# Reordering blocks, transposes, weight loads and the FFN ramp in an attention + softplus-FFN kernel

## Chip, core and metric

The kernel runs on one NeuronCore of a Trainium2 chip. The metric is the device time of one execution in microseconds (us); lower is better. Most executions of one kernel agree within a per cent; the medians below include slow ones. "Span" is the time from the first to the last instruction that the profile records; it is 1.7 to 2.9 us shorter than the device time of the same execution.

Engines: PE is TensorE (PEld its weight loads), DVE is VectorE, ACT is ScalarE, POOL is GpSimd, SP is SyncE, which here only issues DMAs. A trailing q (SPq, POOLq) is that engine's DMA-issuing queue.

## The reference

Attention with 8 heads over 4 sequences of 768 tokens, a causal band of 96 tokens plus 8 global tokens, an ALiBi-like distance bias, then a two-layer FFN with softplus between the layers.

```python
scores = scale * np.matmul(q, k.transpose(0, 1, 3, 2))       # q, k, v: [4, 8, 768, 64] f32
keep = is_global | is_local                                   # 8 globals, 96 back
scores = np.where(keep, scores - slopes * dist, -1e9)
a = softmax(scores)
x = np.matmul(a, v)                                           # -> [3072, 512]
h = x @ w_in                                                  # [512, 2048]
g = np.maximum(h, 0.0) + np.log1p(np.exp(-np.abs(h)))         # softplus
out = g @ w_out                                               # [2048, 512] -> [3072, 512]
```

The kernel works in blocks of 128 tokens (24 in all, 6 per sequence). Block i of a sequence needs the keys and values of blocks i and i-1 and the 8 global tokens of block 0 of the same sequence. Two blocks make one FFN group of 256 tokens; a group has 8 slots, each with eight w_in matmuls of 256 columns ("mm1") and four w_out matmuls of 512 columns ("mm2").

## The kernel before

Loads, casts and the order of the start (cuts are marked):

```python
def load(w):                       # two blocks of one sequence
    nc.sync.dma_start(q32[:], q[b, :, sl, :].rearrange("h (p r) d -> p h (r d)", r=2))
    nc.sync.dma_start(k32[:], k[b, :, sl, :].rearrange("h (p r) d -> p h (r d)", r=2))
    # ... v in four DMAs of 64 partitions

def transp(w, which, psum, eng):   # q and k: eight PE transposes, then one copy
    for r in range(2):
        for m in range(NPAIR):
            nc.tensor.transpose(tr[:, m, r, :], src[:, r, 2 * m : 2 * m + 2, :]..., ident[:])
    cast_on[eng](t[:], psum.rearrange("p (a b t) -> p b a t", b=2, t=64))

def weights(s):                    # DMA with cast f32 -> bf16, issued by GpSimd
    nc.gpsimd.dma_start(w_in_bf[:, :, c], moe_w_in[:, c]...)
    nc.gpsimd.dma_start(w_out_bf[:, f * s : f * s + f, :], moe_w_out[...]...)

load(0); load(1)
# ... biases, casts, transposes, scores of blocks 0 and 1
weights(0)
# ... transposes and scores of blocks 2 and 3
load(2)
for s in range(1, NS):
    weights(s)
load(3)
# ... then one static list: per FFN slot mm1, mm2, and pieces of attention between them
```

x_transp transposes the attention output by four PE transposes per block. All blocks of sequence 0 come first, then those of sequence 1, and so on.

The softmax here doesn't subtract the row's maximum and nothing guards it: scores larger than these inputs give would overflow.

## Time and profile before

The time before is 260.86 us (median of 4; 259.65 to 260.95). The profiled execution had a span of 256.0 us.

From the profile page of the kernel before: busy time, and the rows of the span in 40 slices of 6.4 us. A digit is tenths of the slice that the engine was busy; in the row PEclk it is tenths of full TensorE clock.

```profile
span 256.0 us, 5170 instructions
...
PE 225.1 (88%) x2144; PEld 154.6 (60%) x2144; DVE 139.1 (54%) x279; ACT 156.2 (61%) x201; POOL 34.9 (14%) x66
...
PE   1437687399999999999999999999999999999991
...
PEclk9999999689999999999999999999999999999998
DMA  7999999999965095192291590300202003003033
```

The same kernel in stretches of 20 us; columns are window, its length, busy us of each engine with instruction counts, granted clock, DMA share, GB/s.

```profile
0.00:20.00 20.00, 6.48 (x64) 4.71 (x64) 11.76 (x36) 8.63 (x10) 5.70 (x15) 1.00 1.11 228
20.00:40.00 20.00, 14.85 (x146) 10.64 (x147) 12.08 (x23) 9.91 (x14) 8.10 (x11) 1.00 1.22 217
40.00:60.00 20.00, 13.95 (x123) 9.30 (x122) 6.40 (x13) 8.52 (x12) 3.83 (x7) 0.83 1.18 228
60.00:80.00 20.00, 19.66 (x207) 14.13 (x206) 13.43 (x26) 16.01 (x22) 2.35 (x4) 1.00 0.89 193
```

The chain of waits between 15 and 50 us, in order of time (start, length, what), cut to its two longest pieces:

```profile
23.91 3.47 SPq L102
...
30.44 17.32 DMA v_338<-in_v_dram
```

What to read: from 60 us on PE is full, so there only PE's own work counts. Before 60 us PE was busy for 35.3 of 60 us, part of that at half clock (the clock record shows 0.5 from 46.2 to 53.0 us). The costliest link of the start is one v load, issued at 30.4 us, landing after 17.3 us: it shares the DMA engines with the weights. In the full part two blocks repeat every 17.81 us (mean over the groups from 70.30 to 177.15 us, by the start of each group's first mm1).

### The profile page before, as it was taken

The page shows a single profiled execution, that of the slowest core. Times are in us where ns is not written, and L with a number is a line of the kernel's source. Part 1 is how long each engine was busy: PE and PEld are TensorE (multiplying, and loading weights), DVE is VectorE, ACT ScalarE, POOL GpSimd, SP SyncE. Part 2 cuts the span into 40 slices and gives each one's busy share as a digit, 9 for nine tenths or more (in the row PEclk, how much of TensorE's full clock was granted, in tenths as well). Part 3 has the DMA queues.
Part 4 walks back from the last instruction along what each step waited for, and adds up shares of the span by engine and source line. Part 5 has one row for each costly group of instructions (what it writes and reads, how often), then busy time and mean ns, then how long its engine had stood idle before and what let it go on. Part 6 is the DMA issues. An engine that isn't in the chain of part 4 may idle for free.

```text
span 256.0 us, 5170 instructions
## 1 busy us (share of the span) xinstructions
PE 225.1 (88%) x2144; PEld 154.6 (60%) x2144; DVE 139.1 (54%) x279; ACT 156.2 (61%) x201; POOL 34.9 (14%) x66
## 2 busy tenths in 40 slices
PE   1437687399999999999999999999999999999991
PEld 1324465177667677666776766676676667666640
DVE  6475832246674865764665757746656757430012
ACT  2455544087876767767665777766577677766600
POOL 2142810130300300303001103030000000000000
PEclk9999999689999999999999999999999999999998
DMA  7999999999965095192291590300202003003033
GB/s 188 250 250 199 257 197 199 245 233 240 178 177 105 5 244 86 41 242 48 64 240 30 127 203 0 85 0 22 63 3 65 20 1 86 0 3 82 0 82 82
DMA packets 58391, 29.69 MB, mean 116 GB/s; under 512 B 26624, under 2 KB 55296, under 8 KB 58368
## 3 DMA queue, kind: packets, MB, share of 16 engines
q1 hardware_dynamic: 54144, 25.17, 45.5%
q0 software_dynamic: 4224, 4.19, 9.7%
q8 instruction: 16, 0.26, 0.5%
q14 instruction: 7, 0.06, 0.1%
HBM read 27.26 MB, written 6.29 MB: 131 GB/s over the span
## 4 chain that ended last, share of the span: by engine, by line
PE 79%; DMA 9%; ACT 3%; SPq 3%; DVE 3%; issue 1%; DVEq 0%; POOL 0%; POOLq 0%
PE o_ps_349 L251 17%; PE h_ps_348 L225 16%; PE o_ps_350 L251 16%; PE h_ps_347 L225 15%; DMA v_338<-in_v_dram 7%; PE s_ps L163 4%; PE tr_ps L126 3%; SPq L102 2%; DMA k_84<-in_k_dram 2%; PE tr_ps L214 2%; PE s_ps L165 2%; PE x_ps L195 2%; PE x_ps L198 2%; DVE z L172 1%; ACT g L239 1%
## 5 line engine op out<-in xcount | busy, mean ns | idle before, releaser
L225 PEld LDWEIGHTS <-w_in_bf 128*128 128x128 bf16 x768 | 73.2, 99 | 22.0 <-DVE XT L217 0.7
L172 DVE TENSOR_TENSOR z<-s_ps,biasA 128x1024 f32<-128x1024 f32 x38 | 46.4, 1220 | 26.1 <-PE s_ps L165 26.0
L251 PE MATMUL o_ps_349<-w_out_bf,g 128*128 128x512 bf16 x192 | 57.7, 383 | 1.1 <-ACT g L239 0.7
L251 PE MATMUL o_ps_350<-w_out_bf,g 128*128 128x512 bf16 x192 | 57.6, 382 | 0.0
L179 ACT ACTIVATE pb<-z 128x1024 bf16<-128x1024 f32 (+1 forms) x48 | 46.8, 975 | 14.4 <-DVE z L172 13.2
L237 ACT ACTIVATE e<-h_ps_348 128x512 f32<-128x512 f32 x48 | 28.6, 596 | 40.8 <-PE h_ps_348 L225 40.8
L251 PEld LDWEIGHTS <-g 128*128 128x128 bf16 x384 | 35.1, 98 | 29.8 <-issue 1.7
L225 PE MATMUL h_ps_347<-XT,w_in_bf 128*128 128x256 bf16 x384 | 51.5, 279 | 0.5 <-DVE XT L217 0.5
L239 ACT ACTIVATE g<-e 128x1024 bf16<-128x1024 f32 x48 | 50.7, 1057 | 1.5
L225 PE MATMUL h_ps_348<-XT,w_in_bf 128*128 128x256 bf16 x384 | 50.8, 276 | 0.0
L237 ACT ACTIVATE e<-h_ps_347 128x512 f32<-128x512 f32 x48 | 28.3, 589 | 22.2 <-PE h_ps_347 L225 22.0
L260 DVE COPY osb<-o_ps_349 128x512 f32<-128x512 f32 x12 | 8.3, 692 | 24.1 <-PE o_ps_349 L251 23.6
L202 DVE RECIPROCAL rcp<-x_ps 128x4 f32<-128x4 f32 x46 | 8.1, 176 | 24.4 <-PE x_ps L198 24.4
L203 DVE TENSOR_TENSOR xs<-x_ps,rcp 128x256 bf16<-128x256 f32 x46 | 19.5, 425 | 1.6
L148 POOL COPY kT<-kT 128x32 bf16<-128x32 bf16 x16 | 3.4, 213 | 121.0 <-PE s_ps L165 116.4
L126 PE MATMUL tr_ps<-ident,qb 128*128 128x128 bf16 x96 | 8.6, 242 | 11.7 <-DVE qb L113 11.7
L163 PE MATMUL s_ps<-qT,kT 64*128 64x128 bf16 x180 | 16.2, 231 | 2.8 <-ACT kT L134 2.2
L165 PE MATMUL s_ps<-qT,kT 64*128 64x128 bf16 x152 | 13.8, 228 | 5.5 <-POOL kT L148 5.5
L195 PE MATMUL x_ps<-vb,pb 128*128 128x65 bf16 x156 | 15.5, 198 | 1.3 <-DVE xs L203 1.3
L163 PEld LDWEIGHTS <-kT 64*128 64x128 bf16 x192 | 8.6, 99 | 12.3 <-issue 8.2
L198 PE MATMUL x_ps<-vb,pb 128*128 128x65 bf16 x156 | 15.4, 198 | 0.6 <-DVE vb L154 0.6
L134 DVE COPY qT<-tr_ps 128x1024 bf16<-128x1024 bf16 x11 | 7.6, 692 | 13.3 <-PE tr_ps L126 13.2
(86 smaller groups left out, 181.0 us busy)
## 6 DMA issues: line engine op xcount, KB each, us to landing
out_dram<-osb SPq DMA_DIRECT2D x48, 128.0 KB, 2.4
w_in_bf<-in_moe_w_in_dram POOLq DMA_DIRECT2D x4, 512.0 KB, 11.9
w_out_bf<-in_moe_w_out_dram POOLq DMA_DIRECT2D x4, 512.0 KB, 14.6
q_82<-in_q_dram SPq DMA_DIRECT2D x1, 512.0 KB, 4.2
k_84<-in_k_dram SPq DMA_DIRECT2D x1, 512.0 KB, 6.1
v_86<-in_v_dram SPq DMA_DIRECT2D x4, 128.0 KB, 5.0
q_91<-in_q_dram SPq DMA_DIRECT2D x1, 512.0 KB, 5.5
k_93<-in_k_dram SPq DMA_DIRECT2D x1, 512.0 KB, 7.0
```

Of the source, the lines that this page charges most:

```text
L126: nc.tensor.transpose(tr[:, m, r, :], src[:, r, 2 * m : 2 * m + 2, :].rearrange("p a b -> p (a b)"), ident[:],)
L163: nc.tensor.matmul(psum[:, reg_base(lh), :], kt_of(n)[rows, m, :], qT[rows, m, :])
L165: nc.tensor.matmul(psum[:, reg_base(lh) + 1, :], kt_of(n - 1)[rows, m, :], qT[rows, m, :])
L172: nc.vector.tensor_tensor(z[:], psum[:, :, :], biasA[:, half, :, :], ALU.add)
L179: nc.scalar.activation(pb[:, 0:nr, :], z[:, 0:nr, :], AF.Exp, scale=1.0 / root_d)
L195: nc.tensor.matmul(xv[:, lh, :], pb[:, 2 * j, :], vb_of(n)[:, h, :], start=True, stop=False)
L198: nc.tensor.matmul(xv[:, lh, :], pb[:, 2 * j + 1, :], vb_of(n - 1)[:, h, :], start=False, stop=True)
L203: nc.vector.tensor_tensor(xs[:, 4 * half : 4 * half + 4, :], xv[:, :, 0:D], rcp[:][:, :, None].to_broadcast([P, 4, D]), ALU.mult,)
L225: nc.tensor.matmul(hv[:, j, :], w_in_bf[:, m, fb * P : fb * P + P], XT[:, m, W * g : W * g + W], start=(m == 0), stop=(m == NM - 1),)
L237: nc.scalar.activation(e[:, p % 2, :].rearrange("p (j t) -> p j t", j=2), hv, AF.Exp)
L239: nc.scalar.activation(state["g", g][:, 2 * p - 2 : 2 * p + 2, :].rearrange("p a t -> p (a t)"), e[:].rearrange("p a t -> p (a t)"), AF.Ln ...
L251: nc.tensor.matmul(o_ps[ns][:], gt[:, fb, ns * P : ns * P + P], w_out_bf[:, fb, :], start=(fb == 0), stop=(fb == NFB - 1),)
```

## The change

Its intent: have FFN work for PE early, and take work off PE later.

1. **Block order.** The first blocks of all four sequences lead: they have no predecessor block and give two FFN groups before the rest. Their tokens come in units (sequence 0), (sequence 1), (2 and 3).
2. **Transposes.** q, k and x of the early units stay on PE; later ones are DMA transposes issued by SyncE.
3. **One FIFO ring.** Weights are read as f32 by SyncE into the same 12 raw slots as the tokens, one DMA after another, and GpSimd casts them. Half of each load of the first two units still goes through ScalarE's queue. Loads of later units are held back by manual waits (`gates`) on a given mm1 slot.
4. **mm2 ramp.** The first two groups' mm2 accumulate in three PSUM banks; the later groups use one, and the kernel before used two.
5. **Around it.** A planner fixes the order of every engine from guessed durations; 90 filler matmuls of 256 columns stand where PE would idle at the start; the bias of the first blocks is added by PE; scores of the two head parities alternate.

The core of the diff (a planner of some 130 lines and many renamings are cut):

```diff
+FIRST_UNITS = [[0], [1], [2, 3]]
+FIRST_LOADS = "u0 u1 u2 i0 i1 i2 i3 i4 i5 i6 i7 o0 u3 o1 o2 o3 o4 o5 o6 o7".split()
+FILLERS = 90
+ACT_UNITS = 2
+PE_KEYS = {0: (("s", 2), ("s", 3)), 1: (("s", 2), ("s", 3)), 2: (("s", 2), ("s", 3)), 3: (("s", 0), ("s", 1))}
+PE_X = {0: ("o",), 1: ("o",), 2: ("o",), 3: ("o",), 4: ("x",), 5: ("x",)}
+O_KEYS = {(0, 1): ("s", 3), (1, 0): ("s", 2)}
+ENG_W = {}
 ...
-        nc.gpsimd.dma_start(
-            w_in_bf[:, :, c], moe_w_in[:, c].rearrange("(m p) c -> p m c", p=P)
-        )
+                return nc.sync.dma_start(
+                    raw_t[slot][:].rearrange("p (m c) -> p m c", m=NM),
+                    moe_w_in[:, W * p : W * p + W].rearrange("(m p) c -> p m c", p=P),
+                )
 ...
+        def cast():                               # eng is GpSimd unless ENG_W says otherwise
+                copy_on[eng](w_in_bf[:, :, W * p : W * p + W], raw_t[slot][:]...)
 ...
+            return nc.sync.dma_start_transpose(dst[:, 0 : cols // P, :], src)      # q, k
 ...
+                return nc.sync.dma_start_transpose(dst, xs[:].rearrange("p h d -> p (h d)"))
 ...
-            nc.vector.tensor_copy(vb_of(n - 1)[sl, :, 0:D], vb_of(first)[sl, :, 0:D])
+                nc.gpsimd.tensor_copy(vb_of(prev)[sl, :, 0:D], vb_of(first)[sl, :, 0:D])
 ...
+            if (g, p) in marks:
+                gates[which, i] = [marks[g, p]]   # load of unit i waits for mm1 of group g, slot p
```

## The prediction

> **What bounds the kernel now.** The busy table gives PE 88% of 256.0 us; the measured time is 4.9 us longer. In stretches of 20 us PE is full from 60 to 240 us (19.7 to 20.0). Before that it is busy 6.5, 14.9 and 14.0 us. The chain of waits says why: k load, cast, transpose, bias, one unit after another, then a 17.3 us v DMA landing at 48 us, sharing the engines with weights issued late from GpSimd (17 to 29 us). PE then runs at half clock for some 7 us (clock row 0.6 and 0.8 near 50 us).
>
> Two blocks then repeat every 17.95 us: FFN 8 x (0.87 + 0.87) = 13.9, attention 4.05: q/k transposes 2 x 0.445, x transposes 2 x 0.22, scores about 4 x 0.43, PV. ScalarE has 13.3 us of work in it.
>
> **What changes.**
> - PE loses 144 of 192 q/k and 72 of 96 x transposes: 216 x 0.0555 = 12.0 us. It gains 8 bias matmuls of 512 columns (1.7). Scores of both head parities alternate row halves and share one switch: estimate 2 to 3 less. Sum -13 us, all critical. 90 fillers (0.11 each) fall into start-up idle and hold the clock.
> - Two blocks: 17.95 becomes about 16.4 us; ScalarE at 13.3 (81%) is not yet the bound.
> - 40 DMA transposes join SyncE's queue. The Trainium skill, "DMA: Bandwidth & Descriptors", "Latency and other measured facts", gives them 261 GB/s: about 1 us for 128x1024 bf16; no trace here shows one. The DMA row is at a half near 100 us, a fifth near 200.
> - Start: 3.1 MB for the first blocks, then w_in, one unit, w_out: 13.1 MB in one ring. 512 B packets take 27 to 33 ns per engine (250 to 300 GB/s), weight packets 96 ns per 2 KB read (341 GB/s). So first mm1 at about 16 us, w_in complete at 28, w_out at 42 to 46. Two groups give 1.75 us of PE work per slice of about 1.6 us, so PE stays nearly fed. Instruction order times these durations: 201 us of PE work with switches, 5 of it before the first mm1. Idle until then 11, waits for weights about 5, later holes about 3.
> - Tail: last store split: 4.5 instead of 5.3 us.
>
> 201 + 11 + 5 + 3 + 4.5 = 224 span, + 4.9 = 229; I say **228 us**, 8 in 10 within **220 to 238**. Faster by over 2%: 0.96; within 2%: 0.03; slower: 0.01. Of the 33 us gained, about 13 are PE work, 19 start-up idle and cold clock, 1 tail.
>
> **What would show it.** First w_in matmul at 15 to 18 us; PE full by 30 us without a clock dip; last w_out slice at 41 to 48 us; two blocks every 16.2 to 16.8 us between 80 and 170 us; scores and mm1 waiting under 1 us in total per group on DMA transposes; PE end at 215 to 220.
>
> **What would make it wrong.** DMA transposes slower than estimated (landing 6 us or more, or issue 2 us or more), so that SyncE's in-order queue holds up loads, XT and stores; f32 weights at 250 GB/s; GpSimd weight casts (1.04 us, beside v casts) pacing mm1; ScalarE's exp with permuted output over 0.6 us, making ScalarE the bound; a static order whose guesses miss, with PE holes of 0.5 us per slot.

## The result and the profile after

The changed kernel takes 236.12 us (median of 4 executions: 234.42, 234.59, 237.66 and one of 239.18). Executions over 1.5% slower than the fastest of the same kernel are left out of the means. The ratio to the kernel before is 0.9055, with a 95% interval of 0.8986 to 0.9124. Ratios here are the mean time of one kernel's fast runs over that of the other's fast runs of the same rounds, so they are not quite the ratio of the medians quoted beside them. The change is faster by 9.5%; the predicted 228 us lay 8 us too low, within the range.

The page of the kernel after (slices of 5.8 us):

```profile
span 232.6 us, 5037 instructions
...
PE 214.6 (92%) x1994; PEld 149.0 (64%) x2026; DVE 113.1 (49%) x219; ACT 154.9 (67%) x202; POOL 98.1 (42%) x178
...
PE   8979889898995998999999999999999999999883
...
PEclk9999999999998899999999999999999999999998
DMA  5999999999796449868877545899679422110021
```

The same kernel in stretches of 20 us, columns as before:

```profile
0.00:20.00 20.00, 16.84 (x161) 12.99 (x163) 12.74 (x41) 6.55 (x14) 8.99 (x23) 1.00 0.96 224
20.00:40.00 20.00, 18.07 (x185) 14.47 (x186) 7.75 (x22) 15.29 (x23) 11.58 (x13) 1.00 1.11 344
40.00:60.00 20.00, 18.12 (x153) 11.19 (x154) 10.88 (x19) 10.21 (x13) 16.84 (x27) 1.00 1.03 266
60.00:80.00 20.00, 17.11 (x175) 10.49 (x176) 11.30 (x18) 13.23 (x16) 9.31 (x19) 0.91 0.81 202
```

The 16.84 us of the first stretch are not what they seem: most are fillers. Counting each matmul at the spacing it has at full rate (an estimate of mine: 0.0555 us for 128 columns, 0.109 for 256, 0.2155 for 512, about 0.03 for the small attention ones), PE did 4.4 us of useful work and 9.8 us of filling before 21 us. In the kernel before the same count gives 22.3 us of useful work in the first 60 us; after, 35.8 (two bias matmuls that this trace lacks are counted in). That is the 13.5 us gained at the start.

Three things in the trace stand against the prediction:

- The first mm1 starts at 21.17 us, not at 15 to 18.
- There is a new hole near 70 us, and half clock follows it. The clock record of this execution shows 0.5 from 73.78 to 77.19 us.
- Device time minus span is 1.8 us, not 4.9.

The hole, in the timeline of GpSimd and of PE (start, length, engine, line, operation, tiles; in brackets the idle time before and who ended it). L395 casts loaded rows, L501 copies the values of the global tokens into block n-1's tile, L704 is mm2:

```profile
69.22 0.21 POOL L492 COPY kT<-kTf 128x32 bf16<-128x32 bf16 x1
70.70 1.27 POOL L395 CAST vb<-raw 64x512 bf16<-64x512 f32 x2 [1.27 <-DMA raw<-in_v_dram]
72.01 1.26 POOL L501 COPY vb<-vb 4x512 bf16<-4x512 bf16 x2
73.33 1.27 POOL L395 CAST vb<-raw 64x512 bf16<-64x512 f32 x2
```

```profile
73.53 4.44 PE L704 MATMUL o_ps<-w_out_bf,g 128*128 128x512 bf16 x12
```

The waits of PE between 60 and 80 us in the same kernel (waiting for; us in total, times, longest):

```profile
PE x_ps L601 <- POOL vb L501: 1.3, 1, 1.3
PE x_ps L598 <- ACT g L683: 0.7, 1, 0.7
PE s_ps L546 <- DVE z L572: 0.7, 1, 0.7
```

PE's PV matmuls needed the copy at 72.01, which stood behind a v cast in GpSimd's static order, and that cast waited for a v load that landed at 70.64 us. PE lost 2.7 us in three waits between 69 and 73.3 us; only the last and longest is put down to the copy, the other two to ScalarE and VectorE. Then twelve mm2 matmuls took 4.44 us instead of the 12 x 0.2155 = 2.6 us of full rate.

### The profile page after: what moved, and what is told of

Same layout as the page of the kernel before. It is cut to its first block, busy times and chain, and to the rows that moved or that the text cites. A ratio compares the mean times of both kernels' runs of the same rounds, so it can differ in the third digit from the quotient of the medians.

```text
span 232.6 us, 5037 instructions
## 1 busy us (share of the span) xinstructions
PE 214.6 (92%) x1994; PEld 149.0 (64%) x2026; DVE 113.1 (49%) x219; ACT 154.9 (67%) x202; POOL 98.1 (42%) x178
## 4 chain that ended last, share of the span: by engine, by line
PE 78%; DMA 7%; DVE 4%; POOL 3%; issue 3%; ACT 3%; DVEq 0%; POOLq 0%; ACTq 0%
PE o_ps L704 30%; PE h_ps L657 29%; PE s_ps L546 5%; PE h_ps L807 5%; DMA raw<-in_k_dram 4%; PE s_ps L704 3%; DMA raw<-in_v_dram 3%; PE x_ps L601 2%; ACT pb L581 2%; PE x_ps L598 2%; DVE z L572 2%; POOL vb L501 2%; POOL vb L395 1%; DVE osb L728 1%; PE s_ps L443 1%
## 5 line engine op out<-in xcount | busy, mean ns | idle before, releaser
L657 PE MATMUL h_ps<-XT,w_in_bf 128*128 128x256 bf16 x768 | 95.5, 273 | 1.5 <-POOL w_in_bf L350 0.9
L704 PE MATMUL o_ps<-w_out_bf,g 128*128 128x512 bf16 x323 | 84.8, 385 | 4.0 <-DVE osb L728 1.6
L672 ACT ACTIVATE e<-h_ps 128x512 f32<-128x512 f32 x96 | 59.9, 630 | 30.9 <-PE h_ps L657 30.3
L704 PEld LDWEIGHTS <-g 128*128 128x128 bf16 x384 | 35.9, 99 | 36.2 <-issue 7.0
L581 ACT ACTIVATE pb<-z 128x1024 bf16<-128x1024 f32 x40 | 41.8, 1050 | 18.9 <-DVE z L572 18.8
L395 POOL CAST vb<-raw 64x512 bf16<-64x512 f32 (+1 forms) x60 | 32.8, 547 | 23.1 <-DMA raw<-in_v_dram 17.5
L728 DVE COPY osb<-o_ps 128x512 f32<-128x512 f32 (+1 forms) x23 | 15.2, 665 | 51.4 <-PE o_ps L704 51.3
L395 POOL CAST kb<-raw 64x512 bf16<-64x512 f32 (+1 forms) x44 | 24.0, 545 | 17.5 <-DMA raw<-in_k_dram 15.9
L501 POOL COPY vb<-vb 4x512 bf16<-4x512 bf16 x32 | 19.5, 610 | 17.1 <-PE x_ps L601 16.0
L598 PEld LDWEIGHTS <-pb 128*128 128x128 bf16 x160 | 12.5, 98 | 5.2 <-issue 1.9
L546 PE MATMUL s_ps<-qT,kT 64*128 64x128 bf16 x288 | 13.4, 217 | 0.7 <-DVE z L572 0.7
L601 PEld LDWEIGHTS <-pb 128*128 128x128 bf16 x160 | 11.3, 97 | 3.4 <-issue 1.0
## 6 DMA issues: line engine op xcount, KB each, us to landing
out_dram<-osb SPq DMA_DIRECT2D x23, 256.0 KB, 2.4
```

What stands on the lines that cost most here:

```text
L395: copy_on[eng](dst, src[64 * x : 64 * x + 64, r, :, :])
L501: nc.gpsimd.tensor_copy(vb_of(prev)[sl, :, 0:D], vb_of(first)[sl, :, 0:D])
L546: nc.tensor.matmul(s_ps[:, reg, :].rearrange("p (r t) -> p r t", r=2), kt[rows, m, :], qv(rows, m), start=not biased, stop=True, skip_grou ...
L581: nc.scalar.activation(pb[:, 0:nr, :], src, AF.Exp, scale=1.0 / root_d)
L598: nc.tensor.matmul(xv[:, m, :], pb[:, 2 * m, :], vb_of(n)[:, h, :], start=True, stop=False)
L601: nc.tensor.matmul(xv[:, m, :], pb[:, 2 * m + 1, :], vb_of(prev)[:, h, :], start=False, stop=True)
```

## Experiments

The knobs named in the diffs are constants of the changed kernel. One caution holds for all of them: the order of every engine is planned from durations, so a small edit also moves other instructions. The hole at 70 us hangs on this: between 60 and 84 us PE's longest wait for the global-v copy is 1.04 to 2.72 us with half clock after it in after_again, e2, e3 and e5, and at most 0.3 us, without half clock, in e1, e4, e8 and, with the copies on VectorE, e7 (e11 has no such wait at all, e12 and e13 0.5 us at most). So a run's difference to after_again can hold the worth of the hole beside that of its edit. The first mm1 of group 4 comes at 95.89 us in the kernel after, at 92.24 in e4 and at 92.40 in e7: the hole with its half clock is worth some 3.5 us. All twelve runs gave correct results. "Before" was timed again: 260.09, 260.03, 260.22 and 259.75 us (one execution of it took 577.56 us and is not used).

| run | edit | median us | ratio to before (95%) |
|---|---|---|---|
| after_again | none | 235.92 | 0.9056 (0.9019 to 0.9093) |
| e1_all_pe | all transposes on PE | 246.45 | 0.9480 (0.9447 to 0.9512) |
| e2_one_bank | mm2 ramp in one bank | 234.39 | 0.9007 (0.8964 to 0.9050) |
| e3_no_fill | no fillers | 236.70 | 0.9102 (0.9076 to 0.9128) |
| e4_w_dve | w_out casts on VectorE | 232.14 | 0.8932 (0.8899 to 0.8964) |
| e5_gate | unit 6's v released earlier | 234.83 | 0.9031 (0.8987 to 0.9075) |
| e7_gv_dve | global-v copies on VectorE | 234.71 | 0.9034 (0.8973 to 0.9095) |
| e8_act3 | third unit's loads partly on ScalarE's queue | 236.40 | 0.9105 (0.9060 to 0.9150) |
| e9_no_gate | no manual waits on loads | 259.75 | 0.9995 (0.9964 to 1.0026) |
| e11_swdge | weights by GpSimd's casting DMA | 244.76 | 0.9412 (0.9343 to 0.9482) |
| e12_both | e4 and e7 together | 237.63 | 0.9152 (0.9127 to 0.9176) |
| e13_i_first | e12, two w_in slices ahead of unit 2 | 237.81 | 0.9175 (0.9135 to 0.9214) |

### after_again: how wide is the changed kernel by itself?

No edit.

> The changed kernel once more, beside the others of this call. Both theories: 234 to 239 us, as its four runs gave. It tells how far its own runs spread on this chip, and whether the spread of 2% is of the chip or of the kernel.

Measured 235.92 us; single executions 234.28 to 237.08, and one of 238.0. Their mean clock ranges from 0.982 to 1.0. Of the three longest, two have the lowest clock (0.982) and one the full clock, so half clock explains only a part of the scatter. Differences of about 1 us between edits are therefore not read as effects.

### e1_all_pe: what are the PE transposes worth?

```diff
-PE_KEYS = {0: ..., 1: ..., 2: ..., 3: ...}
-PE_X = {0: ("o",), 1: ("o",), 2: ("o",), 3: ("o",), 4: ("x",), 5: ("x",)}
+PE_KEYS = {i: (("s", 0), ("s", 1)) if i >= 3 else (("s", 2), ("s", 3)) for i in range(15)}
+PE_X = {n: ("o",) if n < 4 else ("x",) for n in range(24)}
-ENG = {}
+ENG = {i: {"k": "POOL"} for i in range(4, 15)}
```

> The changed kernel, but all q, k and x transposes stay on TensorE (k cast whole on GpSimd for the later units). Theory A (TensorE is the bound from 90 us on, so the 216 transposes that left it count in full): 216 x 0.0555 = 12 us more, 246 to 250 us. Theory B (the gain is the start-up alone; the later stretch has slack, and DMA transposes crowd SyncE's queue as much as they save): no more than 3 us from the changed kernel, 234 to 239.

Measured 246.45 us, 10.5 us slower than after_again. Between 80 and 160 us PE is equally full in both kernels; first e1, then the kernel after:

```profile
80.00:160.00 80.00, 78.19 (x858) 57.50 (x870) 55.69 (x106) 59.03 (x75) 26.66 (x49) 1.00 0.36 106
```

```profile
80.00:160.00 80.00, 78.07 (x777) 55.99 (x789) 44.93 (x79) 64.33 (x81) 35.20 (x67) 1.00 0.73 166
```

But two blocks take 17.61 us in e1 (mean from 97.84 to 203.51 us) and 15.98 in the kernel after (95.89 to 191.78 us). The transposes count fully, because there PE is the bound; DMA pays for it with a share that doubles from 0.36 to 0.73, and PE hardly waits for that. The hole at 70 us does not blur this: from the first mm1 of group 4 to the end of the span alone e1 takes 9.8 us longer (146.5 against 136.7). What is left of the gain, 260.09 - 246.45 = 13.6 us, is start-up, tail and a repeat that is 0.2 us shorter than the 17.81 us before (the order of the scores, perhaps; not tested apart).

### e2_one_bank: does the ramp over three banks matter?

```diff
-O_KEYS = {(0, 1): ("s", 3), (1, 0): ("s", 2)}
+O_KEYS = {}
```

> The changed kernel, but mm2 of the first two groups has one bank instead of three. Theory A (start-up is fed by weights that arrive one slice per 1.4 us, and TensorE can only use them at once if several mm2 accumulations are open): 4 to 8 us slower, 239 to 245, with idle TensorE at 30 to 55 us. Theory B (other work fills in, mm1 of group 2 and attention): within 2 us.

Measured 234.39 us, not slower than the changed kernel. Part 4 of the change gives nothing that can be seen; the intervals of the ratio overlap. This run has a hole of its own, where the copies stand behind k casts that wait for a load, with 6.8 us of half clock from 69.53 us on.

### e3_no_fill: do the fillers matter?

```diff
-FILLERS = 90
+FILLERS = 0
```

> The changed kernel without the 90 filler matmuls. Theory A (fillers hold the clock): the first real matmuls and mm1 slices run at half clock[...], 1.5 to 4 us slower. Theory B (39 fillers at half clock, 0.21 us each, stand before the first transposes until 7.7 us and 11 more before the first mm1 at 21.2; the first mm1 waits for its weights in any case): same within 1 us, or up to 1 us faster.

Measured 236.70 us, 0.8 us more. The fillers do what they are for: without them the bias matmul of 512 columns takes 0.58 us instead of 0.38, and the clock record shows no full clock until 23.89 us (5.51 with fillers). In each of the two timelines, first e3_no_fill, then the kernel after, one such line:

```profile
14.29 0.58 PE L527 MATMUL s_ps<-bias,ident 128*128 128x512 bf16 x1 [0.16 <-DVE kTf L465]
```

```profile
14.14 0.38 PE L527 MATMUL s_ps<-bias,ident 128*128 128x512 bf16 x1 [0.98 <-DVE kTf L465]
```

Yet little follows from it. Its first mm1 came at 23.22 us, 2 us later than with fillers; by the first mm1 of group 2 the lag is 0.7 us (57.56 against 56.84). Then its hole at 70 us is longer (a wait of 2.72 us for the copy), and the profiled span is 1.2 us longer than that of after_again and 2.2 longer than that of the kernel after. So the fillers are worth about 1 us, at the edge of the scatter; Theory B is favoured, Theory A not excluded.

### e4_w_dve: is GpSimd the one that is late at 70 us?

```diff
-ENG_W = {}
+ENG_W = {f"o{p}": "DVE" for p in range(8)}
```

> The changed kernel, but the eight f32-to-bf16 casts of w_out run on VectorE (0.69 us estimated) instead of GpSimd (1.04 us). Theory C (GpSimd, full at 16.8 of 20 us from 40 to 60 us, works through w_out late, then k and v casts late, and so makes the hole of TensorE at 69 to 74 us): hole and the half clock of 3.4 us after it shrink or go, 2 to 4 us faster, 232 to 234. Theory D (the hole is made by the loads of unit 6 that reach memory late, v at 70.6 us, whatever GpSimd does): within 1 us of 236, hole still there.

Measured 232.14 us, 3.8 us faster: the interval of the ratio does not touch that of after_again, and this is the fastest kernel. In stretches of 20 us:

```profile
40.00:60.00 20.00, 18.28 (x146) 10.76 (x148) 14.35 (x25) 8.57 (x12) 10.70 (x21) 1.00 1.10 272
60.00:80.00 20.00, 19.25 (x207) 12.55 (x207) 14.43 (x23) 16.53 (x20) 9.71 (x20) 1.00 0.96 226
```

Against the kernel after, GpSimd falls from 16.84 to 10.70 us in 40 to 60, PE rises from 17.11 to 19.25 in 60 to 80, and the clock there goes from 0.91 to 1.00. A w_out cast takes 0.72 us on VectorE and 1.04 us on GpSimd.

But this is not yet Theory C, a GpSimd that has too much to do. In the kernel after it idled 2.79 us and 2.09 us just before the k casts ahead of the hole, the second time for a load:

```profile
66.57 2.58 POOL L395 CAST kb<-raw 64x512 bf16<-64x512 f32 x4 [2.09 <-DMA raw<-in_k_dram]
```

And in e4 the planner, with other durations, put the copies ahead of the v casts:

```profile
67.42 2.57 POOL L395 CAST kb<-raw 64x512 bf16<-64x512 f32 x4
70.06 1.26 POOL L501 COPY vb<-vb 4x512 bf16<-4x512 bf16 x2
71.38 2.57 POOL L395 CAST vb<-raw 64x512 bf16<-64x512 f32 x4
```

The v of unit 6 landed no earlier (70.80 us), but the copies no longer stood behind its casts, and PE waited 0.28 us for them. What took the hole away is this order, not the work taken off GpSimd; the order in e8 is the same.

### e5_gate: or is the load of unit 6's v issued too late?

```diff
+            if g >= 0 and (g, p) not in marks and marks:
+                g, p = max(marks)
             if (g, p) in marks:
```

> The changed kernel, but v loads whose gate does not exist yet wait for the newest mm1 slice instead of being free; two v loads (512 KB each) of units 9 and 10 then no longer stand in SyncE's queue ahead of unit 6's v at 63 us and ahead of unit 7's loads. Theory D (that early load delays unit 6's v by its own 1.7 us and so the hole): v of unit 6 lands 1.5 to 2 us earlier, hole 1 to 2 us smaller, 1.5 to 3.5 us faster with the clock kept. Theory C (GpSimd's own queue): no change in the hole.

Measured 234.83 us. The v of unit 6 landed at 68.88 instead of 70.64 us, but the last wait shrank only from 1.28 to 1.04 us and half clock still followed (73.5 to 76.9). The gain of 1.1 us is within the scatter. The earlier load was no clean test: all four v casts of unit 6 now stood ahead of the copies (69.36 to 71.94 us), where two had, and the copies ran as late as before. An earlier load is not enough while the copies stand behind the casts.

### e7_gv_dve: take only the copies out of GpSimd's order

```diff
-                nc.gpsimd.tensor_copy(vb_of(prev)[sl, :, 0:D], vb_of(first)[sl, :, 0:D])
+                nc.vector.tensor_copy(vb_of(prev)[sl, :, 0:D], vb_of(first)[sl, :, 0:D])
-            op(f"gv{n}.{r}", "POOL", 0.61, ...)
+            op(f"gv{n}.{r}", "DVE", 0.34, ...)
```

> The changed kernel, but the copies of the global keys' v rows (vb to vb, 2 x 0.61 us on GpSimd, in line behind the v casts) go to VectorE as in the kernel before. Theory E (head of line: the copies for block 7 stand behind a cast that waits for unit 6's v until 70.6 us): PV of block 7 starts at once, hole smaller by 1.3 us or more, no half clock, 2 to 4 us faster. Theory D (late loads hold everything): the hole moves a few us later, within 1 us of 236.

Measured 234.71 us (233.58, 233.73, 235.68 and one slow 237.43). In the profiled execution (span 231.5 us) the clock is 1.00 throughout, and the longest wait of PE between 68 and 74 us is 0.35 us:

```profile
60.00:80.00 20.00, 18.94 (x199) 12.00 (x201) 15.99 (x27) 14.92 (x18) 6.19 (x12) 1.00 1.05 217
```

The trace confirms the cause of the hole: the copies behind casts that wait for a load. In the median the gain is 1.2 us, less than e4's and not clearly apart from zero. At the first mm1 of group 4 the profiled execution is 3.5 us ahead of the kernel after, at that of group 11 only 1.1 (204.78 against 205.92): after 92 us PE waits 3.1 us for VectorE's copies out of o_ps, against 1.6.

### e8_act3: share the third unit's loads between two queues

```diff
-ACT_UNITS = 2
+ACT_UNITS = 3
```

> The changed kernel, but the second partition halves of unit 2's loads go through ScalarE's queue as units 0 and 1 do, so both halves of the partitions are written at once. Theory F (512 B packets took 44 ns at 10 to 17 us because each DMA wrote 64 partitions only; they took 31 ns at 3 to 7 us with both queues running): packets of unit 2 at 27 to 35 ns, first w_in slice lands at 16.5 to 17.5 us instead of 18.7, first mm1 at 19 to 20 us instead of 20.8 to 21.2, 1 to 2 us faster. Theory G (512 B packets cost what they cost): 40 ns or more again, first mm1 within 0.5 us of 21.

Measured 236.40 us. The edit failed in its aim: ScalarE issued its half late (9.57, 12.28 and 15.37 us), behind its own waits, the tokens of unit 2 landed up to 25.87 us, and the first mm1 moved from 21.17 to 24.66 us. The total is only 0.5 us longer, but that does not say that a late start is cheap. By the count of useful work, PE is still almost 4 us behind at 60 us; it is level at 80 us because the hole at 70 us was not there. Against e4, which has no hole either, the first mm1 is 3.4 us later, that of group 4 3.9 us (96.12 against 92.24) and the median 4.3 us.

### e9_no_gate: are the manual waits on the loads what makes v late?

```diff
             if (g, p) in marks:
-                gates[which, i] = [marks[g, p]]
+                pass
```

> The edit: the changed kernel without the manual waits that hold the loads of later units until a given w_in slot of PE has run; buffers alone hold them then. Theory F (the throttle causes the loss at 70 us): unit 6's v was issued at 63.98 us, the moment its gating w_in slot began, and landed at 70.64; without the wait it lands before 66 us, the holes of 1.45, 0.89 and 0.67 us before 73 us and the half clock behind them go, time 231 to 234 us, clock 1.0 in 60 to 80 us. Rival (theory C, GpSimd is overloaded at 40 to 60 us and the throttle only follows): SyncE's in-order queue and the raw buffers hold the loads just as long, or the loads crowd the weights in the ring; v of unit 6 lands after 68 us, time 235 to 239 us.

Measured 259.75 us, 24 us slower than the changed kernel; both expectations missed by 20 us or more. SyncE's queue shows why. First e9, then the kernel after, DMA issues of SyncE between 52 and 62 us (L306 loads, L476 transposes, L731 stores):

```profile
52.55 1.02 SPq L306 DMA_DIRECT2D raw<-in_k_dram  x1
53.67 2.19 SPq L306 DMA_DIRECT2D raw<-in_v_dram  x1
...
61.41 3.37 SPq L476 DMA_TRANSPOSE qT<-qb  x1
```

```profile
52.27 1.34 SPq L476 DMA_TRANSPOSE qT<-qb  x1
...
57.36 1.74 SPq L476 DMA_TRANSPOSE kT<-kb  x1
```

Without the waits, six more loads are put ahead of the first DMA transpose. All but the first stretch to 1.0 to 2.2 us each in the queue instead of the usual 0.6, the first q transpose moves from 52.27 to 61.41, the first k transpose from 57.36 to 69.14 us. PE's two largest waits between 60 and 120 us, the second of them for the transposes themselves:

```profile
PE x_ps L598 <- ACT pb L581: 6.6, 4, 2.1
PE s_ps L546 <- DMA kT<-kb: 6.2, 3, 4.8
```

In 80 to 100 us PE is busy for 6.92 of 20 us at a clock of 0.64. So the waits keep loads that nobody needs yet out of an in-order queue that since this change also carries the transposes. The rival named the right queue and was far off in size. Whether the waits also cause the loss at 70 us can't be read from this run: the v of unit 6 did land early (61.46 us), but everything after it is late.

### e11_swdge: what is the FIFO ring of the weights worth?

```diff
-                return nc.sync.dma_start(raw_t[slot][:]..., moe_w_in[:, W * p : W * p + W]...)
+                return nc.gpsimd.dma_start(w_in_bf[:, :, W * p : W * p + W], moe_w_in[...]...)
         ...                      # w_out likewise; the casts on GpSimd are gone
```

> The edit: the changed kernel, but its weights come by GpSimd's own casting DMAs as before the change, in the same slices and order, straight into the bf16 tiles; no f32 slots, no casts of weights on GpSimd, and no common FIFO with the token loads. Theory G (the one FIFO ring is what brings the start): weights now share the DMA engines with the 3.1 MB of the first blocks, so q, k, v of units 0 to 2 land later, first w_in matmul at 24 us or later (21.2 with the FIFO), and the time is 237 to 243 us. Rival H (the order of the bytes hardly counts, since lost start time was absorbed before 80 us in the run with three units' loads on ScalarE's queue; what counts is GpSimd, which loses 16.6 us of weight casts here): first w_in matmul up to 4 us later, but no hole at 70 us, time 231 to 236 us.

Measured 244.76 us, 8.8 us slower. The weights now share the DMA engines from 2.6 us on: the last v of unit 2 lands at 30.87 us (17.39 in the ring), and the first mm1 stands at 37.31 us instead of 21.17. PE's wait, from its timeline:

```profile
31.20 0.27 PE L580 MATMUL x_ps<-vb,pb 128*128 128x65 bf16 x2 [8.54 <-POOL vb L379]
```

And its stretch of 20 to 40 us (PE busy 8.70 us, clock 0.66):

```profile
20.00:40.00 20.00, 8.70 (x79) 6.34 (x76) 5.64 (x15) 1.83 (x4) 9.52 (x17) 0.66 1.23 217
```

But what PE waited for is GpSimd, from its timeline:

```profile
29.57 0.71 POOL L338 DMA_DIRECT2D w_out_bf<-in_moe_w_out_dram  x1 [1.77 <-DMA w_in_bf<-in_moe_w_in_dram]
30.28 6.62 POOL L379 CAST vb<-raw 64x256 bf16<-64x256 f32 x12
```

All sixteen weight issues stand ahead of the first v cast in GpSimd's order, and from 12 us on each waits for an earlier weight slice to land. The v of units 0 and 1, all that the first group needs, had landed by 7.26 and 19.00 us. From 60 us on there is no hole like the one at 70 us. Theory G's time came true, a little beyond its range, but not for its reason alone: the tokens did land later, yet the first mm1 stood behind GpSimd's queue. So the 8.8 us are the worth of taking the weights' issue off GpSimd as a whole; what the order of the bytes is worth by itself was not tested.

### e12_both: do the two reliefs add?

The edits of e4 and e7 together.

> The edit: the changed kernel with both relieving edits at once, the casts of w_out and the copies of the global v rows on VectorE instead of GpSimd. Apart they gave 232.14 and 234.71 against 235.92 us. If both remove one and the same wait (the v cast and copies behind weight casts on GpSimd, 69 to 74 us), the second adds nothing: 231 to 233 us, clock 1.0, no hole over 0.6 us between 60 and 80 us. If they remove different waits the gains add: 229 to 231 us. If VectorE becomes the new queue (it has 14.35 of 20 us of work in 40 to 60 us already with the w_out casts): over 233 us with PE waits on VectorE.

Measured 237.63 us (236.96 to 238.17): slower than either alone, and slower than e4 by 5.5 us. The third case holds: VectorE is the new queue. First e12, then e4, waits of PE between 20 and 240 us:

```profile
PE o_ps L704 <- DVE osb L728: 3.7, 6, 1.3
PE x_ps L598 <- DVE xs L611: 2.0, 1, 2.0
...
PE x_ps L601 <- DVE vb L501: 1.4, 3, 0.8
```

```profile
PE o_ps L704 <- DVE osb L728: 1.6, 2, 0.8
...
PE x_ps L601 <- POOL vb L501: 0.6, 2, 0.3
```

These waits grew by 2.1 + 2.0 + 0.8 = 4.9 us, most of the 6.3 us between the two spans (236.4 and 230.1). VectorE has 16.61 of 20 us of work in 40 to 60 us (14.35 in e4, 10.88 in the kernel after), and between 40 and 120 us a copy of 4 x 512 elements costs it 0.44 us in the mean where the plan had assumed 0.34. The mean hides two cases: 0.28 to 0.29 us where GpSimd casts k or v at no time during the copy, and up to 0.67 us where it does. Since the hole was already gone with the first edit, the second gave nothing and took room on the other engine.

### e13_i_first: is the late first mm1 the weights' doing?

The edits of e12, and:

```diff
-FIRST_LOADS = "u0 u1 u2 i0 i1 i2 i3 ...
+FIRST_LOADS = "u0 u1 i0 i1 u2 i2 i3 ...
```

> The edit: the same as the run with both relieving edits, and the first two w_in slices stand in the ring ahead of the tokens of the third unit (blocks of sequences 2 and 3), which the first FFN group does not need. The w_in slices then land at about 14 and 15.5 us instead of 19.9 and 21.4, and the first w_in matmul can stand at 15 to 17 us instead of 21 to 22. Theory S (the idle start is on the critical path, as the prediction summed it, 1 us for 1 us): 3 to 5 us faster than the run with both edits, 226 to 229 us. Rival T (a late start is absorbed later, because PE is paced until 47 us by the landing of the weights, whose sum of bytes does not change): within 1.5 us of the run with both edits, or slower, since sequences 2 and 3 come 3 us later.

Measured 237.81 us, the same as e12 (ratios 0.9175 and 0.9152, intervals overlapping). That is the time that T named, but S was not tested: the premise was half wrong, and the first mm1 moved by only 1.5 us (21.64 in e12), which the scatter of these runs (235.73 to 239.73) hides. In the two profiled executions e13 stays 1.1 to 2.4 us ahead from the first group to the last. The first w_in slice landed at 11.36 us, 7.4 us earlier than in the kernel after (18.74), and was cast by 12.57 us, but mm1 started only at 20.17 us. PE's timeline and that of VectorE show what it waited for: the attention of the second block.

```profile
17.03 0.22 PE L596 MATMUL x_ps<-vb,pb 128*128 128x65 bf16 x2 [0.23 <-POOL vb L395]
...
18.06 0.42 DVE L611 TENSOR_TENSOR xs<-h_ps,rcp 128x256 bf16<-128x256 f32 x1
...
19.06 0.39 PE L630 MATMUL o_ps<-ident,xs 128*128 128x128 bf16 x4
...
19.48 0.42 DVE L635 COPY XT<-o_ps 128x512 bf16<-128x512 bf16 x1 [0.40 <-PE o_ps L630]
...
20.17 1.04 PE L657 MATMUL h_ps<-XT,w_in_bf 128*128 128x256 bf16 x8
```

One half of that block's v had been issued from ScalarE's queue only at 8.7 us, behind ScalarE's bias work and the landing of its k load, and its cast ran at 16.06 to 16.98 us. From there PV, normalising, transposing and evicting take 3 us. In the kernel after, the same chain ends at 20.12 us (XT written) and the first w_in cast at 20.45; both are there before mm1 at 21.17.

## Why the prediction was right and where it was not

The total was right within the range, 2 us from its upper end, on a sum of which four terms were about right (work, waits for weights, tail, gain of the transposes) and three were off (the start, the later holes, the offset).

| term | predicted | measured in the profiled execution |
|---|---|---|
| PE work with switches | 201 | about 199 (some 193 useful, the 32 matmuls of 512 columns that this trace lacks included, and some 6 of small gaps) |
| idle or filling before the first mm1, beside the work done there | 11 | 16.6 |
| waits for weights | 5 | 6.1 (21 to 47 us) |
| later holes | 3 | 5.5 (69 to 80 us, slow clock included) |
| tail after PE | 4.5 | about 5.0 (a wait of 0.96 us for the last block included) |
| span | 224 | 232.6 |
| device time minus span | 4.9 | 1.8 |

(The measured split is my count, with each matmul at its full-rate spacing; it sums to 232.6 us.)

**Right.** PE's own work was the bound, and what leaves PE in the full part is gained: 10.5 us measured in e1 against the 12 us of transposes removed. Two blocks repeat every 15.98 us, slightly better than the predicted 16.2 to 16.8. The last w_out slice landed at 47.06 us (41 to 48 predicted). The risk in the DMA transposes did not come true while the gates stand: SyncE spends about 1.2 us on each, they land 2.5 to 3.6 us after issue in the median, and no wait of PE for kT or XT is among those of 0.5 us or more (in after_again they sum to 0.9 us over the whole run). The Trainium skill, "DMA: Bandwidth & Descriptors", section "Latency and other measured facts", gives a DMA transpose 261 GB/s (with a non-contiguous middle dimension), which made the prediction's estimate of 1 us per 256 KB. For planning, issue and landing as measured here are the figures that count.

**Step that failed: "first mm1 at about 16 us", and with it the 11 us of idle start.** It took only the loads' bytes into account, and these came later than it said: 512 B packets took 44 ns at 10 to 17 us, not 27 to 33, and the first w_in slice landed at 18.74 us. Beside that stands a path that the sum left out: the attention of the second block, whose v load was issued at 8.7 us by ScalarE, and the chain behind it ends near 20 us whether the weights are there (e13) or not. The mis-sized term is 5.6 us. The runs do not refute summing it 1 to 1. Compared with a run alike in the hole, the lag at the first mm1 is still there at the first mm1 of group 4: 3.4 and 3.9 us (e8 against e4), 16.0 and 12.8 (e11 against e4), -1.5 and -1.6 (e13 against e12). That e8 loses so little in total against the kernel after is due to the missing hole. Each pair differs in more than the start, so this is a reading and not a test.

**Step that failed: "PE full by 30 us without a clock dip", later holes of 3 us.** GpSimd took the weight casts, v casts, k casts and the global-v copies. The prediction named "GpSimd weight casts (1.04 us, beside v casts) pacing mm1" as a risk; GpSimd struck 20 us later, and not through the weight casts, the last of which was done by 50 us, but through copies put behind v casts in GpSimd's static order, which waited for a v load, at the PV matmuls at 70 us. e7 makes the hole vanish by moving the copies; e4, 3.8 us faster, by moving eight casts, after which the planner put the copies first. Behind the hole half clock added 1.8 us (4.44 instead of 2.6).

**Step that failed: the offset of 4.9 us.** It was the difference between the span of one profiled execution (256.0) and the median time of others. Within one execution it is 1.8 us after and up to 2.9 before. The mistake of 3.1 us happened to cover part of the others.

**The split of the gain.** Predicted 13 us PE work, 19 start, 1 tail. Measured 10.5 for the transposes and 13.6 for all else, of which taking the weights' issue off GpSimd is about 9 by e11 (ring and GpSimd's queue not separated), the fillers about 1, the three-bank ramp nothing that can be seen.

The experiments leave a better kernel than both: e4, with w_out cast on VectorE, at 232.14 us (0.8932 of before).

## What to carry to other kernels

Put loads, transposes and stores into one in-order queue only with each load's issue held back to when it is needed: here that hold was worth 24 us, more than any other part. For the first useful matmul follow the whole chain of its slowest input, not the bytes alone. When an edit removes a wait, look in the trace whether it did so by the work moved or by an order that the planner changed along with it: here an order, in e4 and e8. And before moving work to relieve an engine, look at the stretch it lands in, since the same relief given twice cost 5.5 us more than given once.

## What the Trainium skill lacked or had wrong

- "TensorE: Matmul & The Clock Gate", "What's actually happening", says that half clock comes after an idle window of about 3.4 us. The length agrees: the half-clock periods here lasted 3.41 us (73.78 to 77.19) and 6.83 us (46.21 to 53.04 in the kernel before). But no such window was idle: in the 3.41 us before the clock fell PE was busy 1.41 us, with no single wait over 1.3 us. A window that was partly busy was enough here; the page, which elsewhere tells of frequent short idles with the same effect, gives no share for it.
- "DMA: Bandwidth & Descriptors", "Rules for kernel authors", says of two transfers to disjoint partition halves: "Don't bother — they serialize". Here loads of 64 partitions from one queue took 44 ns per 512 B packet (10 to 17 us of the span, 225 GB/s), the two halves in flight from two queues 27 to 31 ns (3 to 7 us, 256 GB/s), and loads of 128 partitions 33 ns (32.5 to 36.5 us, 313 GB/s together with weights in 2 KB packets). So its advice to use 128 partitions fits, and with halves the stretch with two queues was faster; the page has no such figure, and the stretches differ in more than this (e8, which was to test it, failed in its aim).
- For DMA transposes of this size the same page gives a bandwidth; sequencer cycles it has only in its part on trn3. Missing is what sets a plan: about 1.2 us of the issuing queue for each, and 2.5 us (128x512 bf16) to 3.6 us (128x1024 bf16) from issue to landing in the median.
- No page that I used has the time of a small GpSimd copy (there are cycles per element): 4 x 512 bf16 elements take 0.61 us there; on VectorE 0.28 to 0.29 us, and up to 0.72 us where GpSimd casts at the same time (e7). A cast of 128 x 1024 from f32 to bf16 takes 1.04 us on GpSimd and 0.72 on VectorE.
